# First batch of a fused attention and SwiGLU kernel: other PSUM banks for the turned rows and the late o, gates begun inside the fourth row's turn, late statistics moved to just behind the gates

## The chip, the cores and the metric

The kernel runs on one core of one Trainium2 chip. The metric is the device time of one execution in microseconds. The kernel before took 319.64 us in the median of three runs (319.98, 319.64 and 319.4). TensorE is called PE, VectorE DVE, ScalarE ACT, GpSimd POOL and SyncE SP.

## What is computed

Eight batches of eight heads, 576 positions, head size 64, go through a linear attention (no softmax): k and v of a head are multiplied to a 64x64 matrix, q is multiplied with it, each head's row is scaled to unit root mean square and by a gain. The heads are put side by side (512 columns), scaled again by row, and go through a gated layer with 1536 hidden columns.

```python
def _attn_ref(q, k, v, g_norm):
    kv = np.einsum('bhsd,bhse->bhde', k, v)
    out = np.einsum('bhsd,bhde->bhse', q, kv)
    rms = np.sqrt(np.mean(out * out, axis=-1, keepdims=True) + 1e-06)
    return (out / rms * g_norm).astype(np.float32)

def _moe_ref(x, w_gate, w_val, w_out, rms_g):
    rms = np.sqrt(np.mean(x * x, axis=-1, keepdims=True) + 1e-06)
    xn = x / rms * rms_g
    g = xn @ w_gate
    silu = g * (1.0 / (1.0 + np.exp(-g)))
    val = xn @ w_val
    return (silu * val @ w_out).astype(np.float32)
```

## The kernel before

All matrix work is in bf16 with sums in fp32. A batch has 512 main positions, in four chunks of 128 (a chunk is called c), and 64 positions that remain; the remainders of all eight batches make a ninth group. Heads are taken in pairs, so there are four pairs (called j) of 128 columns; `P0` is pairs 0 and 1, `P1` pairs 2 and 3.

The first batch (b = 0) is written out by hand, because everything waits for it. It is cut into an early half (chunks 0 and 1) and a late half (chunks 2 and 3), so that the gated layer can begin with 256 positions while attention goes on with the others. For each half the steps are these:

- q is turned by TensorE (`qT_quads`, `qT_halves`) and copied to `qTs` by ScalarE or VectorE (`qT_out`, L377);
- `oT_mm` (L472) multiplies it with the k-v matrix to the turned attention output; ScalarE squares that (`sqT_`, L483);
- `stat_pairs` (L497) sums the squares over each head with tiny matmuls (4 columns each), and a row of small VectorE steps (`lead_chain` for the early half, `chain`, L562 to L580, for the late half) makes the scale `al` of each row and head;
- `o_pairs` (L439) computes the attention output once more, not turned, and `xna_pairs` (L449, VectorE) scales it;
- `xT_mm` (L621) turns the scaled rows with TensorE's transpose, `xT_out` (L631 on ScalarE, L633 on VectorE) copies them with a gain to `x`. `rows(j, ...)` does both for pair j of the early half.

The gated layer takes `x` in four steps s, one for each pair: a gate is four matmuls that add up in one bank. `gates(0, range(3), 0, 256)` (L775 on) runs the first three gates side by side, all three with step 0, then with step 1, and so on, in two banks of the pool `mm1` and one of `o2`; then ScalarE's silus. `gate_of` and `val_of` (matmuls at L750) do one gate or one value product; the value product's end is VectorE's `h = silu * value` (L770). The list `early` holds these for the first 256 positions: the three gates, values 0 to 2, gates 3 to 5, values 3 to 5, gates 6 to 8, values 6 to 8, and so on. `lead` emits them one by one and calls `behind(n)` after the n-th. The weights come in four blocks of three (`wg[0..3]`, `wv[0..3]`), loaded by the POOL queue in turn, gate and value.

Between these stand the late half's steps. Before the change, `val_of` called `behind_val(j)` between its matmuls and its product: behind value 0 the statistics and their chain, behind value 2 the late o and xna of `P0`. `behind(4)`, after gate 3, did the same for `P1`, and `behind(9)` turned the late rows.

PSUM has eight banks, split into three pools: `mm1` (3), `o2` (2) and `att` (3). A tile takes a bank that was released, in the order of the program, and its first writer waits for that bank's last reader. In the kernel before, row 0 and the late o of `P0` took the two `o2` banks, row 1 and row 3 shared one `att` bank, one after the other, and row 2 took `mm1`.

Every engine takes its own instructions in the order in which they are emitted. From the second batch on, a planner (`Placer`) puts attention's steps into the slots of the gated layer by costs; it and its costs are not touched.

Of the kernel before, what the change touches and what calls it, by code (L numbers as in the profile page):

```python
# [14 lines left out]
OP = mybir.AluOpType  # L15
# [72 lines left out]
def kernel(  # L88
# [12 lines left out]
    nc = tc.nc  # L101
# [31 lines left out]
    o2_p = pool("o2", 2, space=bass.MemoryType.PSUM)  # L133
# [19 lines left out]
    wg = [consts.tile([128, NS, w * 128], BF16, name=f"wg{n}") for n, w in enumerate(FB)]  # L153
    wv = [consts.tile([128, NS, w * 128], BF16, name=f"wv{n}") for n, w in enumerate(FB)]
# [108 lines left out]
    class Att:  # L263
# [58 lines left out]
        def kv_half(self, half):  # L322
            rows, cols = slice(half * D, (half + 1) * D), slice(half * D, (half + 1) * D)
            nc.vector.tensor_copy(out=self.kv[rows, :, half, :], in_=self.kv_ps[rows, :, cols])  # L324

        def qT_quads(self, part, halves, pools):
            tiles = [
                pool.tile([128, 2, MAIN // 2], BF16, name="o2" if pool is o2_p else "att") for pool in pools
            ]
            for c in range(NC):  # L330
                for h in range(H // 2):
                    for ps, hh in zip(tiles, halves):
                        rows, at = slice(hh * D, (hh + 1) * D), slice(h % 2 * D, (h % 2 + 1) * D)
                        nc.tensor.matmul(
                            ps[at, h // 2, c * D : (c + 1) * D],
                            lhsT=mains[0, 0][rows, part, h, c * D : (c + 1) * D], rhs=ident[rows, rows],
                            is_transpose=True, start=True, stop=True, skip_group_check=True,
                        )
            return tiles
# [398 lines left out]
    hs = {}  # L738

    def x_of(g, s, c0, c1):  # L740
        if g == B:
            return xr[:, s, c0:c1]
        cs = slice(c0 // 128, c1 // 128)
        return xs[g][:, s, cs, :] if g < 2 else xs[g][:, cs, s, :]

    def mm1(g, w, j, c0, c1, name="mm1"):
        ps = {"mm1": mm1_p, "o2": o2_p, "att": att_p}[name].tile([128, MAIN], FP32, name=name)
        n, jj = where[j]
        for s in range(NS):
            nc.tensor.matmul(  # L750
                ps[:, : c1 - c0], lhsT=w[n][:, s, jj * 128 : (jj + 1) * 128], rhs=x_of(g, s, c0, c1), start=s == 0, stop=s == NS - 1
            )
        return ps[:, : c1 - c0]

    sis = {}

    def silu_of(g, j, ps, c0, c1):
        sis[g, j] = silu_p.tile([128, MAIN], BF16, name="silu")
        nc.scalar.activation(out=sis[g, j][:, c0:c1], in_=ps, func=ACT.Silu)  # L759

    def gate_of(g, j, c0=0, c1=MAIN):
        silu_of(g, j, mm1(g, wg, j, c0, c1, "o2" if g == 0 and c0 == 0 and j == 5 else "mm1"), c0, c1)

    def val_of(g, j, c0=0, c1=MAIN):
        if (g, j) not in hs:
            hs[g, j] = h_p.tile([128, MAIN], BF16, name="h")
        v_ps = mm1(g, wv, j, c0, c1, {0: "o2", 2: "att", 3: "o2"}.get(j, "mm1") if g == 0 and c0 == 0 else "mm1")
        if g == 0 and c0 == 0:
            behind_val(j)
        nc.vector.tensor_tensor(out=hs[g, j][:, c0:c1], in0=sis[g, j][:, c0:c1], in1=v_ps, op=OP.mult)  # L770

    def slots_a(g, j, c0=0, c1=MAIN):
        return [Slot("gate", lambda: gate_of(g, j, c0, c1)), Slot("val", lambda: val_of(g, j, c0, c1))]

    def gates(g, js, c0, c1):  # L775
        of = [(mm1_p, "mm1"), (mm1_p, "mm1"), (o2_p, "o2")]
        ps = [pool_.tile([128, MAIN], FP32, name=name)[:, : c1 - c0] for _, (pool_, name) in zip(js, of)]
        for s in range(NS):
            for p, j in zip(ps, js):
                n, jj = where[j]  # L780
                nc.tensor.matmul(
                    p, lhsT=wg[n][:, s, jj * 128 : (jj + 1) * 128], rhs=x_of(g, s, c0, c1), start=s == 0, stop=s == NS - 1
                )
        for p, j in zip(ps, js):
            silu_of(g, j, p, c0, c1)
# [97 lines left out]
    V, G, A = nc.vector, nc.gpsimd, nc.scalar  # L883
    H0, H1 = (0, 4), (4, 8)
    P0, P1 = (0, 1), (2, 3)
# [36 lines left out]
    a = Att(0)  # L922
# [7 lines left out]
        a.kv_pairs_out(kva, i, j)  # L930
    idle_on(mains[0, 0][:D, 0, 0:2].rearrange("p h x -> p (h x)"), 1)
    qa, qb = a.qT_quads(0, (0, 1), (att_p, att_p))
    a.qT_out(qa, P0, 0, A)
    a.qT_out(qb, P1, 0, V)
    gT = o2_p.tile([128, NS + 1], FP32, name="o2")
    nc.tensor.matmul(gT, lhsT=grow, rhs=identf, is_transpose=True, start=True, stop=True, skip_group_check=True)
    kvc = a.kv_pairs((2,))
# [10 lines left out]
    for half in range(2):  # L948
        rows = slice(half * D, (half + 1) * D)
        V.tensor_tensor(out=sel[rows, 1, half : half + 1], in0=gcol[rows], in1=gcol[rows], op=OP.mult)  # L950
    V.tensor_scalar(
        out=gain, in0=gall[:, 0:NS], scalar1=gcol, scalar2=float(d_model) ** 0.5, op0=OP.mult, op1=OP.mult
# [12 lines left out]
            a.xna_pairs(o[:, :, 2 * i : 2 * i + 2], (j,), 0, 2)  # L965

    def rows(j, pool_, eng):
        a.xT_mm((j,), (0, 1), ps=xt[j] if j == 0 else a.xT_ps(1, (0, 1), pool_))
        a.xT_out(j, (0, 1), eng)

    xt = [a.xT_ps(1, (0, 1), o2_p)]
    lo = [a.oT_mm(P0, 2, 4, o2_p)]
    rows(0, None, A)
    rows(1, None, A)
    lo.append(a.oT_mm(P1, 2, 4))
    for ps, js in zip(lo, (P0, P1)):
        a.sqT_(ps, js, 2, 4)
    A.preload_act_table(ACT.Silu)
    rows(2, mm1_p, V)
    rows(3, None, V)  # L980

    for t in (0, 2, 1):
        load_cast(1, t, (0, H))
# [11 lines left out]

    half = MAIN // 2
    early = [Slot("half", lambda: gates(0, range(FB[0]), 0, half))]
    for n, w in enumerate(FB):
        js = range(FB0[n], FB0[n] + w)
        early += [slots_a(0, j, 0, half)[0] for j in js if n] + [slots_a(0, j, 0, half)[1] for j in js]  # L1000
    held = {}

    def late_rows(n):
        js = (P0, P1)[n]
        a.xna_pairs(a.o_pairs(js, 2, 4, att_p, "att"), js, 2, 4)

    def behind_val(j):
        if j == 0:
            a.st = None
            a.stat_pairs(P0, 2, 4, att_p, "att")  # L1010
            a.stat_pairs(P1, 2, 4, att_p, "att")
            for f in a.chain(2, NC):
                f()
        if j == 2:
            late_rows(0)

    def behind(n):
        if n == 4:
            late_rows(1)
        if n == 9:  # L1020
            for js in (P0, P1):
                a.xT_mm(js, (2, 3))
                for j in js:
                    a.xT_out(j, (2, 3), A)

    def lead(n0, n1):
        for n in range(n0, n1):
            if n == 12:
                gate = nc.sync.dma_start(out=gbc, in_=g_norm.partition_broadcast(128))
                tc.add_manual_dep(gate.ins, w_loads[-1][0].ins.name, SYNC, reason="the weights come first")  # L1030
            emit([early[n]])
            behind(n)
# [74 lines left out]
```

## Time and profile before

| | |
|---|---|
| median of the runs | 319.64 us (319.4 to 319.98) |
| the profiled execution's own time | 319.01 us |
| its span, from first to last instruction | 317.2 us |
| granted TensorE clock, mean | 1.000 |
| k of the first batch lands at | 7.93 us |
| first gate's matmul starts at | 16.83 us |
| PE is without a pause from | 25.52 us |

The profiled execution is one of many; durations are read from it. A timeline row gives start and length in microseconds, engine, line, operation, tiles written and read, their sizes, the count of instructions put together in the row, and in brackets the idle time of the engine before it with what ended it. Matmuls overlap in a pipeline: each takes a slot of its number of columns and ends some 0.16 us after that slot, so a row of two that shows 0.38 holds PE for 0.22.

### The profile page before, as it was taken

How to read it: one execution, taken by the hardware profiler on the slowest of the kernel's cores; microseconds unless marked ns; L12 is line 12 of the kernel's file. 1: busy time of each engine (PE TensorE's matmuls, PEld its weight loads, DVE VectorE, ACT ScalarE, POOL GpSimd, SP SyncE). 2: the span in 40 equal slices, each digit the busy share in tenths (PEclk: the TensorE clock that was granted, in tenths of full speed). 3: DMA queues.
4: the chain of work that ended last, by engine and by line, in shares of the span. 5: the costliest groups of instructions: out<-in, count | busy, mean ns of one | idle time of the engine just before them, and what ended most of it. 6: DMA issues, size and time to landing. Idle time of an engine off the chain costs nothing.

```text
span 317.2 us, 5713 instructions
## 1 busy us (share of the span) xinstructions
PE 308.0 (97%) x2205; PEld 156.1 (49%) x2226; DVE 168.0 (53%) x378; ACT 139.6 (44%) x264; POOL 87.1 (27%) x108
## 2 busy tenths in 40 slices
PE   7899999999999999999999999999999999999995
PEld 2578855544454445444544444444544444444443
DVE  4674546579759643854196618461769034103310
ACT  2365374596477324631483237322842233233321
POOL 8836430067018302820085008400510000000000
PEclk9999999999999999999999999999999999999999
DMA  8999999999853965595339855964001600040002
GB/s 195 197 203 199 196 238 198 190 217 143 194 177 58 190 156 159 107 192 133 123 98 147 158 147 131 161 139 131 2 0 25 192 1 2 21 106 5 2 33 99
DMA packets 78358, 40.18 MB, mean 127 GB/s; under 512 B 43000, under 2 KB 73852, under 8 KB 78332
## 3 DMA queue, kind: packets, MB, share of 16 engines
q0 software_dynamic: 32304, 14.75, 36.6%
q1 hardware_dynamic: 45328, 24.48, 30.9%
q10 hardware_dynamic: 700, 0.59, 0.6%
q8 instruction: 17, 0.28, 0.4%
q14 instruction: 9, 0.07, 0.1%
HBM read 37.78 MB, written 9.44 MB: 149 GB/s over the span
## 4 chain that ended last, share of the span: by engine, by line
PE 93%; DMA 2%; DVE 2%; issue 1%; ACT 1%; SPq 0%
PE mm L750 57%; PE o L788 27%; DMA stg<-in_k_dram 2%; PE mm L788 2%; PE att L294 2%; PE o L422 1%; PE att L422 1%; DVE h L770 0%; PE mm L312 0%; PE att L621 0%; ACT x L631 0%; PE mm L819 0%; PE o L819 0%; PE att L472 0%; PE o L750 0%
## 5 line engine op out<-in xcount | busy, mean ns | idle before, releaser
L770 DVE TENSOR_TENSOR h<-silu,mm 128x512 bf16<-128x512 bf16 (+1 forms) x117 | 74.3, 636 | 88.0 <-PE mm L750 79.1
L759 ACT ACTIVATE silu<-mm 128x512 bf16<-128x512 f32 (+1 forms) x118 | 65.7, 560 | 83.8 <-PE mm L750 73.4
L750 PE MATMUL mm<-x,wv 128*128 128x512 bf16 (+1 forms) x418 | 97.8, 358 | 0.2
L750 PE MATMUL mm<-x,wg 128*128 128x512 bf16 (+1 forms) x414 | 97.3, 358 | 0.2
L788 PE MATMUL o<-wo,h 128*128 128x512 bf16 x382 | 87.5, 379 | 1.1 <-issue 0.6
L750 PEld LDWEIGHTS <-wv 128*128 128x128 bf16 x480 | 46.4, 98 | 45.7 <-issue 0.5
L750 PEld LDWEIGHTS <-wg 128*128 128x128 bf16 x468 | 45.5, 98 | 46.2 <-issue 0.2
L514 POOL TENSOR_TENSOR sq<-sq,g 128x512 bf16<-128x512 bf16 x28 | 32.0, 1154 | 127.5 <-ACT sq L405 81.9
L788 PEld LDWEIGHTS <-h 128*128 128x128 bf16 x420 | 40.3, 98 | 47.0
L808 ACT COPY osb<-o 128x512 f32<-128x512 f32 x33 | 19.3, 587 | 69.1 <-PE o L788 66.2
L522 DVE TENSOR_REDUCE st<-sq 128x8 f32<-128x512 bf16 x56 | 35.9, 678 | 0.0
L324 DVE CAST kvs<-att 64x256 bf16<-64x256 f32 x14 | 5.9, 422 | 30.7 <-PE att L294 30.5
L591 DVE TENSOR_TENSOR xna<-outa,al 128x512 bf16<-128x512 bf16 x24 | 15.1, 682 | 0.0
L750 PE MATMUL mm<-xr,wv 128*128 128x512 bf16 x47 | 12.3, 379 | 0.1
L750 PE MATMUL mm<-xr,wg 128*128 128x512 bf16 x47 | 12.3, 379 | 0.1
L229 POOL CAST main_q<-stg 128x1024 bf16<-128x1024 f32 x10 | 10.2, 1068 | 0.0
L908 ACT ACTIVATE wv<-wv,gain 128x384 bf16<-128x384 bf16 x16 | 9.0, 607 | 0.4 <-PE mm L750 0.4
L200 POOL DMA_DIRECT2D vc<-in_v_dram x10 | 8.5, 859 | 2.1 <-PE att L359 1.1
L788 PE MATMUL mm<-wo,h 128*128 128x512 bf16 x23 | 7.4, 379 | 0.2 <-issue 0.2
L459 ACT ACTIVATE sq<-att 128x512 bf16<-128x512 f32 x12 | 7.6, 630 | 0.0
L459 ACT ACTIVATE sq<-o 128x512 bf16<-128x512 f32 x12 | 7.3, 610 | 0.0
L200 POOL DMA_DIRECT2D kc<-in_k_dram x7 | 6.5, 933 | 2.7 <-DMA kc<-in_k_dram 1.6
(150 smaller groups left out, 186.9 us busy)
## 6 DMA issues: line engine op xcount, KB each, us to landing
out_dram<-osb SPq DMA_DIRECT2D x27, 256.0 KB, 2.5
stg<-in_q_dram SPq DMA_DIRECT2D x6, 1024.0 KB, 7.5
vc<-in_v_dram POOLq DMA_DIRECT2D x7, 512.0 KB, 8.1
kc<-in_k_dram POOLq DMA_DIRECT2D x7, 512.0 KB, 6.2
out_dram<-osb SPq DMA_DIRECT2D x17, 128.0 KB, 2.4
wg<-in_moe_w_gate_dram POOLq DMA_DIRECT2D x4, 384.0 KB, 10.2
wv<-in_moe_w_val_dram POOLq DMA_DIRECT2D x4, 384.0 KB, 11.4
wo<-in_moe_w_out_dram POOLq DMA_DIRECT2D x4, 384.0 KB, 14.4
```

The lines of the kernel that those rows point to most:

```text
L200: return nc.gpsimd.dma_start(out=to[:, heads[0] : heads[1], : NC * D], in_=view)
L229: return copy(out=mains[b, t][:, cs[0] : cs[1], h0:h1, :], in_=staged[b, t].rearrange("p h (c d) -> p c h d", c=NC)[:, cs[0] : cs[1], h0:h ...
L459: nc.scalar.activation(out=self.sq[c][:, 0], in_=self.o_of(c), func=ACT.Square)
L514: eng.tensor_tensor(out=self.sq[c][:, 1], in0=self.sq[c][:, 0], in1=g2, op=OP.mult)
L522: nc.vector.reduce_sum(out=self.part(self.st[:, which], c), in_=of, axis=AX.X)
L591: return eng.tensor_tensor(out=self.part(self.xna, c), in0=of, in1=self.part(self.al, c).to_broadcast([128, 2, H // 2, D]), op=OP.mult,)
L750: nc.tensor.matmul(ps[:, : c1 - c0], lhsT=w[n][:, s, jj * 128 : (jj + 1) * 128], rhs=x_of(g, s, c0, c1), start=s == 0, stop=s == NS - 1)
L759: nc.scalar.activation(out=sis[g, j][:, c0:c1], in_=ps, func=ACT.Silu)
L770: nc.vector.tensor_tensor(out=hs[g, j][:, c0:c1], in0=sis[g, j][:, c0:c1], in1=v_ps, op=OP.mult)
L788: nc.tensor.matmul(ps, lhsT=hs[g, j][:, t * 128 : (t + 1) * 128], rhs=wo[j // OB][:, j % OB, :], start=j == 0, stop=j == NF - 1)
L808: (eng.copy if eng is nc.scalar else eng.tensor_copy)(out=o, in_=ps)
L908: A.mul(out=w[:, s], in_=w[:, s], mul=gain[:, s : s + 1])
```

## The change

Five things are changed, all in the first batch's early part:

- The two copies of the early q swap engines: the half for `P0` goes to VectorE, that for `P1` to ScalarE.
- Rows 0 and 1 both take `o2` banks; the late o of `P0` takes an `att` bank in place of `o2`, and stands behind row 0.
- Row 3 is no longer turned ahead of the gates but inside `gates`, after the three matmuls of step 0.
- The statistics of the late half and their chain stand right behind the gates, ahead of value 0's matmuls. The late o and xna of `P0` stand behind value 2's matmuls as before, but value 2's product on VectorE is held back (`held`) until xna of `P1` has been emitted.
- Gate 7 of the early half takes an `o2` bank (gate 5 already did).

```diff
     def gate_of(g, j, c0=0, c1=MAIN):
-        silu_of(g, j, mm1(g, wg, j, c0, c1, "o2" if g == 0 and c0 == 0 and j == 5 else "mm1"), c0, c1)
+        silu_of(g, j, mm1(g, wg, j, c0, c1, "o2" if g == 0 and c0 == 0 and j in (5, 7) else "mm1"), c0, c1)
 
     def val_of(g, j, c0=0, c1=MAIN):
...
-        v_ps = mm1(g, wv, j, c0, c1, {0: "o2", 2: "att", 3: "o2"}.get(j, "mm1") if g == 0 and c0 == 0 else "mm1")
-        if g == 0 and c0 == 0:
-            behind_val(j)
-        nc.vector.tensor_tensor(out=hs[g, j][:, c0:c1], in0=sis[g, j][:, c0:c1], in1=v_ps, op=OP.mult)
+        leads = g == 0 and c0 == 0
+        v_ps = mm1(g, wv, j, c0, c1, {0: "o2", 2: "att", 3: "o2"}.get(j, "mm1") if leads else "mm1")
+
+        def product():
+            nc.vector.tensor_tensor(out=hs[g, j][:, c0:c1], in0=sis[g, j][:, c0:c1], in1=v_ps, op=OP.mult)
+
+        if leads and j == 2:
+            held["product"] = product
+        else:
+            product()
...
         for s in range(NS):
+            if s == 1:
+                rows(3, None, V)
             for p, j in zip(ps, js):
...
-    a.qT_out(qa, P0, 0, A)
-    a.qT_out(qb, P1, 0, V)
+    a.qT_out(qa, P0, 0, V)
+    a.qT_out(qb, P1, 0, A)
...
     def rows(j, pool_, eng):
-        a.xT_mm((j,), (0, 1), ps=xt[j] if j == 0 else a.xT_ps(1, (0, 1), pool_))
+        a.xT_mm((j,), (0, 1), ps=a.xT_ps(1, (0, 1), pool_))
         a.xT_out(j, (0, 1), eng)
 
-    xt = [a.xT_ps(1, (0, 1), o2_p)]
-    lo = [a.oT_mm(P0, 2, 4, o2_p)]
-    rows(0, None, A)
-    rows(1, None, A)
+    rows(0, o2_p, A)
+    lo = [a.oT_mm(P0, 2, 4)]
+    rows(1, o2_p, A)
     lo.append(a.oT_mm(P1, 2, 4))
...
     rows(2, mm1_p, V)
-    rows(3, None, V)
...
-    def behind_val(j):
-        if j == 0:
+    def behind(n):
+        if n == 0:
             a.st = None
             a.stat_pairs(P0, 2, 4, att_p, "att")
             a.stat_pairs(P1, 2, 4, att_p, "att")
             for f in a.chain(2, NC):
                 f()
-        if j == 2:
+        if n == 3:
             late_rows(0)
-
-    def behind(n):
         if n == 4:
             late_rows(1)
+            held.pop("product")()
```

## The prediction, made before the changed kernel ran

> **What bounds the kernel now.** I read the page first, then the busy time by stretches of the span, then the chain of waits from 14 to 40 us, then the timeline of the four engines over the same stretch, and last the landings of the loads. The page says TensorE:
>
> ```profile
> span 317.2 us, 5713 instructions
> ...
> PE 308.0 (97%) x2205; PEld 156.1 (49%) x2226; DVE 168.0 (53%) x378; ACT 139.6 (44%) x264; POOL 87.1 (27%) x108
> ...
> PE 93%; DMA 2%; DVE 2%; issue 1%; ACT 1%; SPq 0%
> ```
>
> The share is an average. The next two rows are of the busy time by stretches (first the stretch and its length, then PE, PEld, DVE, ACT, POOL busy with counts, then the granted clock, the DMA share, GB/s):
>
> ```profile
> 14.40:25.52 11.12, 9.72 (x101) 7.82 (x99) 7.71 (x27) 8.26 (x20) 5.75 (x10) 1.00 1.31 203
> 25.52:39.20 13.68, 13.68 (x130) 12.09 (x132) 6.69 (x16) 5.87 (x16) 7.23 (x11) 1.00 1.45 197
> ```
>
> From 25.52 us on PE is full. Ahead of that, where the change works, it idles 11.12 - 9.72 = 1.40 us, and every microsecond taken out there moves the rest of the kernel forward, unless a load is late. The chain names who ends those waits (start, length, engine, tile, line):
>
> ```profile
> 16.72 0.27 PE att L621 x2
> ...
> 18.30 0.44 PE o L750 x4
> 18.74 0.19 PE att L497 x8
> ...
> 18.96 0.18 DVE u L562
> ...
> 21.42 0.42 DVE h L770
> ...
> 21.89 0.60 PE o L750 x4
> ...
> 23.61 1.08 DVE h L770 x3
> ...
> 25.52 13.70 PE mm L750 x124
> ```
>
> Read it so: the fourth row (L621) comes late, the gates follow it, then the first value product (L750, 0.44), then the statistics (L497), which start a run of twelve small VectorE steps; only behind them stands the first h (21.42), whose bank the fourth value product (21.89) wants. Later VectorE, then ScalarE, hold PE until 25.52.
>
> **The change part by part.** All times below are of the profiled execution. Lags come from the rows: about 0.03 from PE's end to ScalarE or VectorE, 0.05 back; a 256-column matmul takes 0.44/4 = 0.11, so a group of four 0.44 and twelve gates 1.31; a 128-column one half.
>
> *The swapped q copies.*
>
> ```profile
> 10.87 0.59 ACT L377 COPY qTs<-att 128x512 bf16<-128x512 bf16 x1 [3.11 <-PE att L334]
> 10.90 0.42 DVE L377 COPY qTs<-att 128x512 bf16<-128x512 bf16 x1 [0.42 <-PE att L334]
> 11.51 0.38 PE L472 MATMUL o<-qTs,kvs 128*128 128x256 bf16 x2
> 11.94 0.27 PE L472 MATMUL o<-qTs,kvs 128*128 128x256 bf16 x1
> ```
>
> ScalarE ends at 11.46 and PE starts the first o 0.05 later. With VectorE on that half the copy ends at 11.32 and PE starts at 11.37: 0.14 gained. The bounds are 0 (PE is held by the products ahead) and 0.17 (the two durations' difference); I take 0.14, because 11.46 + 0.05 is just when PE starts. The other half now ends at 11.49, still ahead of its reader at 11.94 - 0.14. Statistics, scale and xna of the first half follow in a chain without slack, so I move all of them by 0.14.
>
> *Rows and gates.*
>
> ```profile
> 15.03 1.42 DVE L449 TENSOR_TENSOR xna<-att,al 128x256 bf16<-128x256 f32 x4
> 15.51 0.28 PE L621 MATMUL o<-ident,xna 128*128 128x128 bf16 x2
> 15.83 0.47 ACT L631 ACTIVATE x<-o,gain 128x256 bf16<-128x256 bf16 x1 [0.23 <-PE o L621]
> 16.20 0.47 ACT L631 ACTIVATE x<-att,gain 128x256 bf16<-128x256 bf16 x1
> 16.49 0.35 DVE L633 TENSOR_SCALAR x<-mm,gain 128x256 bf16<-128x256 bf16 x1
> 16.56 0.60 ACT L483 ACTIVATE sqT<-o 128x512 bf16<-128x512 f32 x1
> 16.83 0.38 PE L781 MATMUL mm<-x,wg 128*128 128x256 bf16 x2
> 17.04 0.61 ACT L483 ACTIVATE sqT<-att 128x512 bf16<-128x512 f32 x1
> 17.66 1.28 ACT L978 ACT_TABLE_LOAD   x1
> ```
>
> Before, row 3 took the bank of row 1 and so waited for ScalarE's second x (16.20 + 0.47 = 16.67; PE at 16.72), and all gates stood behind it. After, rows 0 and 1 have the two o2 banks, row 3 one that only needs its own data, and the first gate of each of the three banks asks for x of row 0 alone. Worked forward: xna ends at 15.31, 15.64, 15.98, 16.31 (15.03 - 0.14, 0.33 apart, 0.42 long); row 0 on PE 15.37 to 15.65; ScalarE's x0 15.69 to 16.16, x1 0.37 behind it, to 16.53; gates of step 0 from 16.20, three of them; row 3 16.53 to 16.81; step 1 at 16.64 (x1 is there), step 2 at 16.97 (x2, 16.35 + 0.35), step 3 at 17.30 (x3, 16.84 + 0.35 = 17.19). The last gate is issued by 17.62. So the gates begin 16.83 - 16.20 = 0.63 earlier, of which 0.14 is the copy, and give 0.11 back for row 3's two transposes. The weight changes around these have no row; bounds are 0 and two loads, 0.2, and I take 0, since PEld overlaps PE throughout.
>
> *Statistics ahead of the first value product.* They need both late squares: ScalarE's order stays x0, x1, square, square, so the second ends at 16.42 + 0.48 + 0.61 = 17.51, in time for 17.62. Statistics then end at 17.62 + 0.16 (a matmul's tail) + 0.19 = 17.97 and VectorE starts at 18.00 in place of 18.96: 0.96 = 0.14 + 0.38 + 0.44 for the value product taken out of the way. The table load moves with the squares to 17.52, the first silu to 18.80; the first h comes later than that and hides it.
>
> *The late half on VectorE.*
>
> ```profile
> 22.09 0.68 DVE L449 TENSOR_TENSOR xna<-att,al 128x512 bf16<-128x512 f32 x1
> 23.20 0.39 PE L621 MATMUL att<-ident,xna 128*128 128x128 bf16 x4
> 23.62 1.57 ACT L631 ACTIVATE x<-att,gain 128x256 bf16<-128x256 bf16 x4 [1.63 <-PE att L621]
> 23.98 2.13 PE L750 MATMUL mm<-x,wg 128*128 128x256 bf16 x16
> 25.06 1.47 ACT L759 ACTIVATE silu<-mm 128x256 bf16<-128x256 f32 x4
> ```
>
> The small steps take 21.42 - 18.96 = 2.46, so h 0 is 20.46 to 20.87, and value 3 could start at 20.92. PE by itself gets there at 17.62 + 0.19 + six groups of 0.44 + two late o of 0.22 = 20.89. Then h 1, xna of the first pair 21.13 to 21.81, and now at once xna of the second, 0.60 behind: 22.41, because h 2 stands behind it. PE's late turns at 22.26 and 22.48 wait for neither; before, the second waited. Held back, h 2 starts at 22.33 and h 3, 4, 5 follow 0.33 apart, the last until 23.73. The next gates that take their banks come at 23.8 and 24.2, so some 0.4 of cover is left; without it PE would wait for that rest. Gate 7 in an o2 bank waits for a silu in place of h 4. ScalarE takes the late x from 22.26 + 0.39 + 0.03 = 22.68; its silus start 1.44 behind, the third of them (0.36 apart, 0.38 long) ends at 24.12 + 0.72 + 0.38 = 25.22, and the second gate of the second half, which takes its bank, starts at 25.27. Before, that gate stood eight matmuls into the full stretch, at 25.52 + 0.88 = 26.40: 1.13 gained.
>
> *The loads.* No DMA is added, removed or moved on any queue, so landings stay put while PE comes nearer. Issue times and delays, of wg 1 to 3, of wv 1 alone, and of the last values' piece for batch 2:
>
> ```profile
> L248 POOL DMA_DIRECT2D wg<-in_moe_w_gate_dram x3: 760/780/797, 10.1 to 13.0; - x3
> ...
> DMA to landing us min/median/max: 9.1/11.4/13.8
> ```
>
> ```profile
> L249 POOL DMA_DIRECT2D wv<-in_moe_w_val_dram x1: 770/770/770, 10.8 to 10.8; - x1
> ...
> DMA to landing us min/median/max: 10.1/10.1/10.1
> ```
>
> ```profile
> L196 POOL DMA_DIRECT2D vc<-in_v_dram x1: 692/692/692, 42.5 to 42.5; - x1
> ...
> DMA to landing us min/median/max: 15.6/15.6/15.6
> ```
>
> ```profile
> 11.51 0.78 POOL L248 DMA_DIRECT2D wg<-in_moe_w_gate_dram  x1
> 59.17 0.82 PE L294 MATMUL att<-vc,kc 128*64 128x64 bf16 x40
> ```
>
> wg 1 lands at 19.2, wanted after the change at 17.62 + 0.19 + 1.32 + 0.22 = 19.35. wv 1 lands at 20.9: value 3 at 20.95, a gain of 0.94 there. wg 2 lands at 11.51 + 11.4 = 22.9, so gate 6 starts at 22.95 and not 22.70: 23.98 - 22.95 = 1.03. The values' piece lands at 58.1 and is wanted eight matmuls into the row at 59.17, 0.15 later: no gain past 59.32 - 58.15 = 1.17 survives this place.
>
> **Sum.** By the weights' gate 1.03, by ScalarE's silus 1.13; I take the middle, 1.07 (to 0.01, by hand). The profiled execution took 319.01 us, span 317.2 and 1.81 around it; it becomes 317.94. The runs' median is 319.64, 0.63 over it, so the same step gives 319.64 - 1.07 = **318.6 us**.
>
> **The rivals.**
> *Loads clip the gain.* The early start is real, but wg 2 or the values' piece lands some 0.3 to 0.7 later against PE than in this one execution, and PE waits. For it: the room left is 0.15, 0 and 0, where 0.7 to 1.1 was before, and the DMA share is above 1 in both stretches. Against: the landings follow each other on a full queue, and nothing of this change touches it. Gain 0.4 to 0.8, 319.0, about half of it within 0.2%.
> *The gates do not begin early.* ScalarE's x0, or PE's order, holds step 0 until row 3 is turned, and the swap is covered. Then only the statistics' place is left, 0.44: 319.2. For it: PE takes its queue in order, so any late x between the steps stops all. Against: the x times above, each 0.03 or more ahead of use.
> *Slower, by the clock.* The denser mix of transposes, tiny statistics and half-filled steps from 14 to 25 us lets the granted clock fall there. Price: the stretch's 9.72 us of PE at clock c costs 9.72/c - 9.72; the gain is eaten at 0.90, and below 0.85 (1.72) the kernel is slower than can be told from no change; at 0.75 it is 3.24 - 1.07 slower, 321.8. Against: the clock is 1.00 in the same stretch, which already has these transposes and more idle time.
> The Trainium skill, "TensorE: Matmul & The Clock Gate", Part 4, says that transposes do not count as PE work for the clock gate as matmuls do, which is this rival's rule; this trace shows 1.00 with them, so it does not bear it out.
>
> **How the numbers follow.** Forecast 0.66, loads 0.18, no early gates 0.08, clock 0.08. What a measurement of this kernel can tell from no change is 0.2%, 0.64 us. Faster is the forecast and half of the loads' case, 0.75; within is the other half and the third, 0.17; slower 0.08. The range starts from the gains 1.17 and 0.4 (318.5 and 319.2) and adds the spread of the runs' median, about 0.3 either way (319.4 to 319.98), with 0.2 more below for the lags: 318.0 to 319.5.
>
> **What would show it.** In the changed profile: PE's first o near 11.37; the first gates at 16.2 with row 3's turn inside them; VectorE's u at 18.0; value 3 at 20.95; gate 6 at 22.95, its wait ended by a DMA or not at all; no wait for VectorE ahead of the second late turn; PE full from about 25.3, and the second batch's values product near 58.1 without a wait. A u later than 18.5, a wait of PE on h 4 or 5, a wait on a load over 0.3 us, or a clock under 1.00 would make the prediction wrong.

## The result, and the profile after

The changed kernel took 317.78 us in the median of seven runs (317.57 to 318.6), the kernel before 319.34 us in the median of seven beside them (318.76 to 319.98). The ratio is 0.9957 with an interval of [0.9943, 0.9972]: 1.56 us or 0.49% less, more than the 0.2% that can be told from no change. The profiled execution took 317.84 us, 1.17 less than the 319.01 of the one before. The forecast was 318.6, and the time lies below its range.

The page of the kernel after, its span, its busy times and its chain's shares by engine:

```profile
span 316.1 us, 5734 instructions
...
PE 309.8 (98%) x2226; PEld 156.0 (49%) x2226; DVE 167.8 (53%) x378; ACT 139.5 (44%) x264; POOL 87.1 (28%) x108
...
PE 92%; DMA 5%; POOL 1%; issue 0%; DVE 0%; ACT 0%; POOLq 0%
```

The span is 1.1 shorter, and VectorE and ScalarE have left the chain that this page counts. The stretch ahead of the full one, by busy time (columns as before):

```profile
14.40:25.52 11.12, 10.31 (x107) 8.68 (x108) 7.54 (x28) 8.56 (x21) 5.57 (x9) 1.00 1.31 203
```

PE idles 11.12 - 10.31 = 0.81 us there, where it idled 1.40, and that although 0.62 of the 0.81 (14.40 to 15.02) lies ahead of the first row. The chain of waits of the kernel after, from 14 to 40 us, shows who ends the rest:

```profile
10.16 10.84 DMA wv<-in_moe_w_val_dram
...
21.04 0.61 PE o L750 x4
...
22.98 0.61 PE mm L750 x4
```

The chain goes back from the fourth value product (21.04) to a load, wv 1, issued at 10.16, landed at 21.00. Ahead of that load the chain names nothing in this execution. Its timeline, by row (start, length, engine, line, tiles, sizes, count, idle time before with what ended it):

```profile
15.02 0.28 PE L621 MATMUL o<-ident,xna 128*128 128x128 bf16 x2 [0.90 <-DVE xna L449]
15.86 0.38 PE L789 MATMUL mm<-x,wg 128*128 128x256 bf16 x2
16.19 0.27 PE L621 MATMUL att<-ident,xna 128*128 128x128 bf16 x2
17.66 0.17 DVE L562 TENSOR_SCALAR u<-att 128x16 f32<-128x16 f32 x1 [0.81 <-PE att L497]
21.04 0.61 PE L750 MATMUL o<-x,wv 128*128 128x256 bf16 x4 [0.19 <-DMA wv<-in_moe_w_val_dram]
22.36 0.61 PE L621 MATMUL att<-ident,xna 128*128 128x128 bf16 x8
22.79 1.57 ACT L631 ACTIVATE x<-att,gain 128x256 bf16<-128x256 bf16 x4 [1.51 <-PE att L621]
22.98 0.61 PE L750 MATMUL mm<-x,wg 128*128 128x256 bf16 x4
25.23 0.60 PE L750 MATMUL mm<-x,wg 128*128 128x256 bf16 x4
```

The gates begin at 15.86 with row 3's turn (16.19) inside them; the statistics reach VectorE at 17.66; the eight late turns (22.36) go through without a wait; ScalarE's late x start at 22.79 and the second gate of the second half at 25.23. One thing grew: PE idles 0.90 us ahead of row 0, where it idled 0.54 ahead of the late o before.

Another execution of the same kernel, taken with e18_after, had v's last load later (11.67 in place of 11.18). The chain of waits of e18_after:

```profile
15.50 0.28 PE o L621 x2
...
20.76 0.92 PE o L750 x8
...
23.02 0.44 PE mm L750 x4
...
23.89 14.19 PE mm L750 x128
```

Here no load stands in the chain: from row 0 at 15.50 on it names PE alone. But a pause of PE shorter than 0.16 us lies under the modelled end of the matmul before it, and neither the busy time nor the chain shows it. The starts in the timeline of e18_after do:

```profile
22.81 1.57 ACT L631 ACTIVATE x<-att,gain 128x256 bf16<-128x256 bf16 x4 [1.19 <-PE att L621]
23.73 1.04 PE L750 MATMUL mm<-x,wg 128*128 128x256 bf16 x8
24.25 0.40 ACT L759 ACTIVATE silu<-mm 128x256 bf16<-128x256 f32 x1
24.71 0.60 PE L750 MATMUL mm<-x,wv 128*128 128x256 bf16 x4
24.78 0.69 ACT L759 ACTIVATE silu<-mm 128x256 bf16<-128x256 f32 x2
25.25 0.60 PE L750 MATMUL mm<-x,wg 128*128 128x256 bf16 x4
```

Eight matmuls from 23.73 hold PE until 24.60, and the next starts at 24.71, 0.06 behind the first silu (24.25 + 0.40); four from 24.71 hold it until 25.15, and the second gate of the second half starts at 25.25, 0.05 behind the third silu (24.78 to 25.20). So ScalarE ends the last two waits, 0.11 and 0.10. In the nine profiled executions of the changed kernel and its versions below that keep gate 7's bank and had no fall of the clock, this gate starts 2.43 to 2.45 behind ScalarE's first late x, whatever the head and the loads did. The changed kernel thus reaches its late turns by PE's own work when its head is late (22.39) and behind wv 1 when its head is early (22.36), ScalarE's silus set the start of the gate behind them, and both executions have the same span of 316.1 us.

### The profile page after: what moved, and what is told of

Same layout as the page of the kernel before. It is cut to its first block, busy times and chain, and to the rows that moved or that the text cites. A ratio compares the mean times of both kernels' runs of the same rounds, so it can differ in the third digit from the quotient of the medians.

```text
span 316.1 us, 5734 instructions
## 1 busy us (share of the span) xinstructions
PE 309.8 (98%) x2226; PEld 156.0 (49%) x2226; DVE 167.8 (53%) x378; ACT 139.5 (44%) x264; POOL 87.1 (28%) x108
## 4 chain that ended last, share of the span: by engine, by line
PE 92%; DMA 5%; POOL 1%; issue 0%; DVE 0%; ACT 0%; POOLq 0%
PE mm L750 58%; PE o L796 27%; DMA wv<-in_moe_w_val_dram 3%; DMA vc<-in_v_dram 2%; PE mm L796 2%; PE att L294 2%; PE o L422 1%; PE att L422 1%; PE att L621 0%; PE mm L827 0%; PE o L827 0%; PE o L750 0%; PE att L397 0%; PE att L472 0%; POOL remv L895 0%
## 5 line engine op out<-in xcount | busy, mean ns | idle before, releaser
L796 PE MATMUL o<-wo,h 128*128 128x512 bf16 x396 | 89.9, 379 | 0.0
```

Of the source, the lines that this page charges most:

```text
L796: nc.tensor.matmul(ps, lhsT=hs[g, j][:, t * 128 : (t + 1) * 128], rhs=wo[j // OB][:, j % OB, :], start=j == 0, stop=j == NF - 1)
```

## The experiments

In some runs the mean granted clock reads 0.995 or less. Two of them were profiled, and in both the clock had fallen for one or two stretches of 3.41 us in the first 20 us (a fall, below). These runs are counted apart in this table, since they are mostly 1 to 4 us longer. Each block of rows shares its runs of the kernel before.

| kernel | all runs, median us | clock 0.997 or more: median us | runs under 0.997 |
|---|---|---|---|
| before (beside e1 to e4) | 318.98 | 318.98 | 0 of 35 |
| e1_after | 318.60 | 317.75 | 6 of 12 |
| e2_swap | 318.96 | 318.94 | 1 of 11 |
| e3_stats | 318.32 | 318.31 | 2 of 11 |
| e4_rows | 318.36 | 318.33 | 1 of 12 |
| before (beside e5 to e8) | 319.06 | 319.06 | 0 of 34 |
| e5_spin | 318.07 | 317.98 | 1 of 10 |
| e6_spin_late_w | 318.22 | 318.22 | 0 of 11 |
| e7_before_late_w | 319.13 | 319.13 | 0 of 11 |
| e8_spin_split | 317.98 | 317.98 | 0 of 12 |
| before (beside e9 to e12) | 319.06 | 318.90 | 8 of 35 |
| e9_after | 318.32 | 318.04 | 4 of 12 |
| e10_spin_no_swap | 317.87 | 317.87 | 0 of 12 |
| e11_spin_no_hold | 318.01 | 317.96 | 1 of 12 |
| e12_spin_no_gate7 | 318.17 | 318.17 | 0 of 12 |
| before (beside e13 to e15) | 318.85 | 318.85 | 1 of 29 |
| e13_spin_before | 318.91 | 318.91 | 0 of 11 |
| e14_spin_rows | 318.57 | 318.57 | 0 of 11 |
| e15_spin_stats | 318.44 | 318.44 | 0 of 12 |
| before (beside e16 to e18) | 318.88 | 318.86 | 2 of 26 |
| e16_late_o_first | 318.31 | 318.07 | 4 of 12 |
| e17_filler_one | 317.98 | 317.98 | 0 of 8 |
| e18_after | 317.88 | 317.87 | 3 of 12 |

### The change whole, and its parts

e1_after is the changed kernel once more, beside three kernels with one part of the change each.

> The whole change again, beside the kernel before on the same chip. Theory (the terms are right, the miss came from carrying one execution's distance to a median of other runs): 1.07 us less than the kernel before, between 0.9 and 1.25, and the profiled execution shows the fourth value product waiting for the weights of block 1. Rival (the gain is larger than the summed terms, because the kernel before is also held by something that the profiled execution did not show): 1.35 us or more less.

Without falls it is 318.98 - 317.75 = 1.23 us less than the kernel before; with them the ratio is 0.999 [0.9973, 1.0007]. The six runs with a fall have a median of 319.49, 1.74 more than the other six. Its profile caught one (mean clock 0.995; two stretches by busy time, then PE's timeline):

```profile
11.92:15.33 3.41, 2.29 (x37) 1.58 (x35) 2.20 (x11) 1.87 (x6) 2.93 (x5) 1.00 1.31 203
15.33:18.74 3.41, 3.36 (x20) 2.60 (x21) 1.68 (x5) 2.88 (x6) 1.16 (x2) 0.50 1.32 204
```

```profile
15.38 0.39 PE L621 MATMUL o<-ident,xna 128*128 128x128 bf16 x2 [0.89 <-DVE xna L449]
16.84 0.63 PE L789 MATMUL mm<-x,wg 128*128 128x256 bf16 x2
```

The granted clock is 0.50 for 3.41 us from 15.33, and two gates' matmuls take 0.63 where they took 0.38. It begins where the idle piece ahead of row 0 ends, behind a stretch in which PE worked 2.29 of 3.41 us.

e2_swap has the swapped copies alone, in the kernel before.

```diff
-    a.qT_out(qa, P0, 0, A)
-    a.qT_out(qb, P1, 0, V)
+    a.qT_out(qa, P0, 0, V)
+    a.qT_out(qb, P1, 0, A)
```

> The kernel before with only the two q copies swapped between ScalarE and VectorE. Theory: 0.14 us less (the copy ends 0.14 earlier and everything behind it follows), bounds 0 and 0.17. Rival (part of the larger gain comes from here): 0.3 us or more less.

Its ratio is 1.0002 [0.9991, 1.0012]: no change, but 0.14 us would lie inside that interval too, so the timeline has to decide. That of e2_swap:

```profile
11.03 0.38 PE L472 MATMUL o<-qTs,kvs 128*128 128x256 bf16 x2
11.45 0.38 PE L312 MATMUL mm<-vc,main_k 128*128 128x128 bf16 x4
13.24 0.26 DVE L540 RECIPROCAL r<-mm 128x16 f32<-128x16 f32 x1 [0.58 <-PE mm L497]
```

and of the kernel before:

```profile
11.51 0.38 PE L472 MATMUL o<-qTs,kvs 128*128 128x256 bf16 x2
11.72 0.38 PE L312 MATMUL mm<-vc,main_k 128*128 128x128 bf16 x4
13.52 0.26 DVE L540 RECIPROCAL r<-mm 128x16 f32<-128x16 f32 x1 [0.49 <-PE mm L497]
```

Behind the first o PE multiplies the last heads' k and v (L312). That load landed at 11.41 in e2_swap and at 11.68 in the kernel before, and both times L312 starts 0.04 later and the first statistics step (r) 1.79 to 1.80 behind L312. In e2_swap PE was done with the first o at 11.03 + 0.22 = 11.25 and waited 0.20 for the load. An earlier q copy moves only the o in front of that wait.

e3_stats has the late statistics behind the gates alone, e4_rows the banks and row 3 inside the gates alone.

> The kernel before with only the late statistics and their chain moved from behind the first value product's matmuls to behind the gates. Theory: the chain's first step on VectorE comes 0.44 us nearer to the gates, the fourth value product follows it, 0.44 us less in all. Rival: more than 0.6 us less, or nothing, if the wait at the fourth value product is taken by something else.

> The kernel before with only the other banks for the rows and the late o, and row 3 turned inside the gates. Theory: the wait of row 3 for the second x of ScalarE is gone, two transposes are inside the gates: 0.32 to 0.38 us less. Rival (no early start, because the late o now waits for the second copy of ScalarE and holds the rows): 0 to 0.1 us less.

Ratios 0.9985 [0.9974, 0.9995] and 0.9987 [0.9977, 0.9998]. From r to u, where the statistics reach VectorE, the profiled executions take 5.44 us before (13.52 to 18.96), 5.00 in e3_stats and 5.08 in e4_rows: 0.44 and 0.36 less, as forecast. The medians, 0.67 and 0.65 under the kernel before, looked too large for that; e13 to e15 return to them.

### Does a filled idle piece keep the clock up, and do the loads decide?

e5_spin puts three matmuls that compute nothing into PE's idle piece ahead of row 0.

```diff
     oy = a.o_pairs(P1, 0, 2, att_p, "att")
+    spin(mm1_p.tile([128, MAIN], FP32, name="mm1"), 3)
```

> The changed kernel with three more 512-column matmuls into a bank of their own, behind the first half's last o and ahead of row 0's turn, where PE idles 0.90 us. Theory (the falls of the granted clock come from that idle piece): the runs have no fall, mean granted clock 0.999 or more, about 1.2 us less than the kernel before (ratio 0.996). Rival (the falls come from the mix of small matmuls as a whole): in a third to a half of the runs the mean granted clock is still near 0.995 and these are some 1.7 us longer. Third: the added matmuls end after row 0 is ready and cost what they stick out, up to 0.3 us, with no fall.

One run of ten fell (0.989); the others lie 1.08 under the kernel before. The filler pushes nothing back: row 0 starts 2.00 behind the first statistics step r in its profile (13.80 to 15.80), as in the kernel after (13.02 to 15.02).

e6_spin_late_w and e7_before_late_w delay the weights in e5_spin and in the kernel before, e8_spin_split brings their first columns early.

```diff
-    w_loads = [load_w(n) for n in range(len(FB))]
+    w_loads = [load_w(0)]
+    load_cast(1, 2)
+    w_loads += [load_w(n) for n in range(1, len(FB))]
...
-        if t:
+        if t == 1:
             load_cast(1, t)
```

> The kernel of e5_spin with one 64 KB piece of v's load moved ahead of the weights of pieces 1 to 3 on POOL's queue, so that these land later. Theory (the weights' landings set the end of the changed kernel): value 3 and gate 6 start as much later as wv 1 and wg 2 land, about 0.3 to 0.6, and the time is 0.3 to 0.6 us over e5_spin. Rival (VectorE's and ScalarE's chain sets it): within 0.1 of e5_spin.

> The kernel before with the same piece of v's load moved ahead of the same weights. Theory (in the kernel before the weights have 0.7 to 1.1 us of room): within 0.1 us of the kernel before, with no wait of PE on wv 1 or wg 2. Rival (the weights already decide there): 0.3 to 0.6 us slower.

> The kernel of e5_spin with the first 128 columns of wg 1, wv 1 and wg 2 loaded by transfers of their own ahead of the rest. Theory (these landings are the last thing that holds PE): value 3 starts when PE itself gets there, 0.1 to 0.2 earlier, and the time is 0.1 to 0.3 us under e5_spin. Rival (VectorE's held product or ScalarE's silus take their place): within 0.1. Against both: the extra transfers delay the later weights and the time is 0.1 to 0.4 over e5_spin.

Later weights cost the changed kernel 318.22 - 317.98 = 0.24, a little less than expected, and the kernel before 0.07. In the profiled execution of e7_before_late_w PE did wait for wv 1 and for wg 2, 0.2 us each, which had not been expected there; that cost the runs nothing that can be told. The chain of waits of e6_spin_late_w goes back to wg 2:

```profile
12.20 11.10 DMA wg<-in_moe_w_gate_dram
23.30 0.04 issue
23.34 0.61 PE mm L750 x4
```

Earlier weights bring nothing (317.98 both), as the rival had it: in the profiled executions of e5_spin and e8_spin_split no load ends a wait of PE behind row 0, and the two last pauses, 0.11 each, are those behind ScalarE's silus, as in e18_after. Where the weights are not delayed, a load ends a wait of some length only in executions whose head is early.

### The clock again, and the smaller parts

e9_after repeats the changed kernel on another chip; e10 to e12 take one part out of e5_spin each: the swap, the held product, gate 7's bank.

> The changed kernel once more, beside the kernel before on another occasion than e1_after. Theory (the idle piece ahead of row 0 lets the clock fall, whenever the clock's own period ends badly for it): two to six of some twelve runs at a mean granted clock of 0.995, these 1.5 to 1.9 us longer than the others; the others 1.1 to 1.3 less than the kernel before. Rival (the falls were those of one chip on one occasion): none, all runs between 317.5 and 318.1.

> The kernel of e5_spin with the two q copies on their old engines. Theory (PE's products behind the first o wait for v's last load, so an earlier q copy gains nothing): first late o 0.14 later, the rest the same, within 0.1 us of e5_spin, 0.9 to 1.1 less than the kernel before. Rival (the prediction's chain without slack): 0.14 slower than e5_spin.

> The kernel of e5_spin with the third value product issued by VectorE in its old place, between the two late xna. Theory (gate 6 waits for wg 2 and so has 0 to 0.3 of cover): the second late turn waits 0.3 on VectorE and the loss is 0 to 0.2 us. Rival (no cover): the second late turn and all behind it are 0.3 to 0.4 later, and so is the end.

> The kernel of e5_spin with gate 7 back in the bank that it had. Theory (its bank comes free with a held value product, some 0.3 late): gate 7 waits up to 0.3 on VectorE and the time is 0.1 to 0.3 us over e5_spin. Rival (ScalarE's silus hold the next gates for as long): within 0.1.

Four runs of e9_after fell, as expected, but here the kernel before fell too, in 8 of 35; and the runs without a fall gained 0.86, less than expected. e5_spin itself did not run on this chip: it lies 1.08 under its kernel before. The three versions here lie 1.03, 0.94 and 0.73 under theirs (318.90). So the swap is again worth nothing that can be told, the held product some 0.1 (in e11_spin_no_hold the second late turn waits 0.2 for VectorE, where 0.3 was expected), and gate 7's bank about 0.3 (318.17 - 317.87 = 0.30 beside e10_spin_no_swap); these are differences of medians, without intervals of their own. PE's timeline of e12_spin_no_gate7, where the first value product of that place starts at 25.12,

```profile
22.84 2.44 PE L750 MATMUL mm<-x,wg 128*128 128x256 bf16 x16
25.12 0.60 PE L750 MATMUL mm<-x,wv 128*128 128x256 bf16 x4
```

and of e10_spin_no_swap, where it starts at 24.64:

```profile
22.88 0.61 PE L750 MATMUL mm<-x,wg 128*128 128x256 bf16 x4
23.33 0.60 PE L750 MATMUL o<-x,wg 128*128 128x256 bf16 x4
23.77 1.04 PE L750 MATMUL mm<-x,wg 128*128 128x256 bf16 x8
24.64 0.60 PE L750 MATMUL mm<-x,wv 128*128 128x256 bf16 x4
```

### The two parts without falls between them

> The kernel before with the three matmuls of e5_spin in the same place. Theory (they only fill an idle piece of PE): the median within 0.2 us of the kernel before, no run under a mean granted clock of 0.997 where the kernel before beside it has some. Rival (they push row 0 back, as their end lies 0.1 to 0.3 past its data): 0.1 to 0.3 slower.

> The kernel of e4_rows (other banks, row 3 inside the gates) with the three matmuls of e5_spin. Theory (the prediction's terms): 0.3 to 0.4 us less than the kernel of e13_spin_before. Rival (the single part brings what the medians of e4_rows showed): 0.6 to 0.7 less.

> The kernel of e3_stats (late statistics ahead of the first value product) with the three matmuls of e5_spin. Theory (the prediction's terms): 0.4 to 0.5 us less than the kernel of e13_spin_before. Rival (the single part brings what the medians of e3_stats showed): 0.6 to 0.7 less, and with e14_spin_rows 1.2 to 1.4 together.

The filler itself does nothing to the kernel before: 318.91 against 318.85, ratio 1.0001 [0.9992, 1.001]. Against e13_spin_before the rows bring 0.34 and the statistics 0.47; the intervals of these kernels against the kernel before are some 0.3 and 0.45 us either way. Those are the prediction's terms (0.38 and 0.44), and the 0.65 and 0.67 of the earlier medians did not come again; why those were larger stays open.

### Who makes the falls?

> The changed kernel with the late o of the first two pairs ahead of row 0 again, as in the kernel before, in its new bank; nothing is added. Theory (the change makes PE's idle piece longer by putting this o behind row 0, and a fall follows a period of 3.41 us with too little PE work): the idle piece splits, the emptiest 3.41 us of PE ahead of 16 us have 2.5 us of work in place of 2.24, and of some twelve runs none or one falls under a mean granted clock of 0.997; row 0 and all behind it start no later; 0.9 to 1.2 us less than the kernel before. Rival (row 0 waits for the o): 0.1 to 0.2 longer than the runs of e18_after without a fall. Rival (the place of the o has nothing to do with falls): as many falls as in e18_after.

```diff
-    rows(0, o2_p, A)
     lo = [a.oT_mm(P0, 2, 4)]
+    rows(0, o2_p, A)
```

> The changed kernel with one matmul of 512 columns in the place of e5_spin's three. Theory (a threshold in PE's work in a period): the emptiest 3.41 us have about 2.5 us of work, and the falls are as rare as in e16_late_o_first. Rival (only a filled idle piece helps): a third of the runs fall, as in e18_after.

> The changed kernel, beside e16_late_o_first and e17_filler_one on the same chip. Theory: a quarter to a half of the runs at a mean granted clock of 0.995 or less, these 1.5 to 2 us longer; the others 0.9 to 1.2 less than the kernel before. Rival (the falls belong to single chips): none.

e16_late_o_first went the rival's way. Its timeline:

```profile
14.12 1.05 ACT L377 COPY qTs<-att 128x512 bf16<-128x512 bf16 x2
15.22 0.38 PE L472 MATMUL att<-qTs,kvs 128*128 128x256 bf16 x2 [1.04 <-ACT qTs L377]
15.44 0.39 PE L621 MATMUL o<-ident,xna 128*128 128x128 bf16 x4
```

The o starts 0.05 behind the second of ScalarE's two copies (14.12 + 1.05 = 15.17), though its own q is the first: in its new place it waits for the `att` bank that the second copy reads. So the idle piece becomes 1.04, row 0 starts 2.36 behind r (13.08) in place of 2.00, the time without falls is 0.20 over e18_after, and four of twelve runs fall. With its banks the change was right to put row 0 first. The emptiest 3.41 us of PE in the stretch ahead of the gates (from 10.5 us on), by busy time, in e16_late_o_first, in the kernel after, in e17_filler_one and in the kernel before:

```profile
11.80:15.21 3.41, 2.15 (x36) 1.64 (x36) 2.30 (x11) 2.08 (x6) 2.60 (x4) 1.00 1.32 203
```

```profile
11.60:15.01 3.41, 2.24 (x37) 1.58 (x35) 2.24 (x11) 2.00 (x6) 2.77 (x5) 1.00 1.30 200
```

```profile
11.55:14.96 3.41, 2.46 (x38) 1.66 (x38) 2.38 (x11) 2.06 (x6) 2.41 (x4) 1.00 1.31 197
```

```profile
13.35:16.76 3.41, 2.56 (x38) 1.64 (x38) 2.71 (x10) 2.11 (x6) 2.05 (x3) 1.00 1.32 203
```

These figures are each of one execution. The runs with a fall, whatever its place, are 4 of 12 at 2.15, 13 of 43 at 2.24 (the seven runs of the result had none), 0 of 8 at 2.46 and 11 of 159 at 2.56. The parts do not fit as well: e4_rows, at 2.24 too, fell in 1 of 12, and e2_swap, e3_stats and e7_before_late_w, at 2.55 to 2.56, in 3 of 33. The clearest comparison is the filler: the changed kernel and its versions with one or three matmuls of it fell in 2 of 77 runs, the changed kernel without it in 13 of 43.

## Why the prediction was wrong, step by step

*The gain was read about right, in part by luck.* The sum was 1.07. Without falls the changed kernel lies 1.23, 0.86 and 0.99 under the kernel before in the three repeats, 1.03 in the mean, and the profiled execution that the sum was made against became 317.84, where 317.94 was worked out. The sum took the middle of two waits that stand one behind the other (gate 6 by the weights 1.03, the second gate of the second half by ScalarE's silus 1.13; their middle is 1.08). The later one decides: that gate, at 26.40 before and forecast at 25.27, came at 25.23, 1.17 earlier, and at 25.25 in e18_after. That it came so near is luck: the late turns were 0.10 to 0.13 later than forecast (22.36 and 22.39 for 22.26), and the silus stood 0.26 apart where 0.36 was taken.

*The step that failed is the last of the sum:* "The runs' median is 319.64, 0.63 over it, so the same step gives 319.64 - 1.07 = 318.6". The median of the kernel before is 318.85 to 319.06 in five other sets of 26 to 35 runs, and 319.34 in the result's seven, of which the first three were the shown ones. So the profiled 319.01 was the typical execution, and the three runs stood high. Taken from 319.01 the sum gives 317.94, 0.16 over the measured 317.78. The spread of 0.3 added below the range was too small for this 0.63. Why the three runs stood high is open: neither their profiles nor their clocks are on record, so a late head or a fall of the clock may have made them (the kernel before with a fall took 319.41 to 322.61).

A late head need not carry over to the changed kernel. The step r starts at 13.02 in the profiled execution of the result and at 13.51 in that of e18_after, 0.49 later, and both spans are 316.1. In e13_spin_before, r is 0.37 later than in the kernel before (13.89) and the span 0.4 longer (317.6). But there are only a few such pairs, and the medians do not say how much of the runs' scatter the change takes up.

*The swapped q copies, 0.14:* wrong, nothing of it is seen (e2_swap, e10_spin_no_swap), the lower bound given, though for another reason: the chain behind the o was taken as one "without slack", and holds a wait for v's last load. The term is missing where it should be: in e18_after, whose head stands as in the kernel before (r at 13.51 and 13.52), the gates begin at 16.35 and u comes at 18.15, both 0.15 later than forecast.

*Rows and gates, 0.38 beyond the swap:* 0.36 from r to u, 0.34 in time. *Statistics, 0.44:* 0.44 and 0.47. Both together shorten r to u from 5.44 to 17.66 - 13.02 = 4.64, by 0.80 where 0.82 was forecast. That u came at 17.66 and not at 18.00 in the execution of the result is its early head.

*The late half:* the second late turn waits no more, as forecast; holding the product is worth some 0.1. Gate 7's bank, priced only as part of the chain to 25.27, is worth about 0.3.

*The loads:* value 3 was forecast at 20.95 and came at 21.04 behind wv 1, gate 6 at 22.95 and came at 22.98 behind wg 2. PE stood 0.34 ahead of value 3 (20.26 + 0.44 = 20.70 to 21.04), a little over the 0.3 that the prediction had named as a sign of being wrong; the 0.19 of the row leaves out the modelled end. As a rival, that the loads clip the gain, they cost 0.24 only where e6_spin_late_w delayed them. The values' piece of batch 2 clipped nothing.

*Slower, by the clock:* given 0.08, it came in 13 of 43 runs, and in none of those that gave the result. Its price was right: the stretch from 14.40 to 25.50 shows a clock of 0.85 in e1_after, for which the prediction's formula gives 1.72, and 1.74 was measured. Its place was wrong, as far as the runs show: a filler in the emptier piece of PE ahead of row 0 took nearly all falls away, though the dense mix from 14 to 25 us behind it stayed. Which part of the change makes the falls is not shown: e4_rows has the same idle piece and fell in 1 of 12, and e16_late_o_first did not make the piece shorter. The Trainium skill, "TensorE: Matmul & The Clock Gate", Part 1, describes a free-running window of 3413 ns and a clock of either half or full rate, and these runs agree: 3.41 us, 0.50 and 1.00. Its rule there, under "HAM oscillation", to leave no idle gap of PE over some 3.4 us, is not enough here: the longest idle piece in the period ahead of the fall is 0.89 us.

## What to carry to other kernels

Before a distance between one profiled execution and a short median is carried into a forecast, run the kernel before more often and ask which of the two is typical: three runs stood 0.6 to 0.8 over the usual median here. A distance that a late transfer makes may not carry over either, where the change moves the end to something else. Pauses of PE shorter than a matmul's modelled end are read from the starts, not from the busy time. A part that is hidden must be followed to the next thing that its consumer waits for; here the o came earlier and the next products' load did not. Where a change opens an idle piece of PE ahead of dense work, try to fill it (one or three idle matmuls): the changed kernel with such a filler, and without the swap, had no fall in twelve runs, where the changed kernel beside it had four. Its ratio to the kernel before, 0.9955 [0.9933, 0.9976], flatters it, since eight of those 35 runs had a fall; without them it is 318.90 - 317.87 = 1.03 us less.

## What had not been expected of the hardware

Both falls that were profiled came behind a period of 3.41 us in which PE had little work, without one long pause: 2.29 us of it in e1_after and 2.34 in e11_spin_no_hold (periods are counted from the first boundary in the clock record of each execution). But no threshold follows from that. In e3_stats a period with 2.34 was followed by no fall, and in e16_late_o_first not even one with less:

```profile
14.05:17.46 3.41, 2.25 (x25) 1.86 (x23) 2.37 (x7) 2.83 (x7) 1.62 (x3) 1.00 1.32 205
17.46:20.87 3.41, 3.41 (x42) 2.99 (x41) 2.42 (x13) 2.70 (x7) 0.84 (x2) 1.00 1.31 201
```

This measure counts the modelled end of each matmul as work. With 0.16 us taken off each, the periods ahead of the two falls are the emptiest in the first 24 us of all twenty profiled executions, about 1.4 and 1.55 us against 1.7 or more; that was worked out from the traces after the runs, rests on two falls, and no run tests it. The first boundary lies at another point of every execution (3.9 to 7.2 us), which would explain why the same kernel falls in some runs only; that is not shown. In e11_spin_no_hold the fall began in the head, ahead of the filler and of the rows, and lasted two periods (by busy time):

```profile
7.96:11.37 3.41, 2.34 (x49) 1.54 (x48) 1.05 (x4) 0.40 (x1) 2.61 (x4) 1.00 1.43 187
11.37:14.78 3.41, 3.24 (x28) 2.48 (x28) 1.10 (x6) 1.55 (x4) 3.02 (x5) 0.50 1.30 199
14.79:18.20 3.41, 3.41 (x31) 2.22 (x29) 2.44 (x9) 1.29 (x3) 1.76 (x2) 0.50 1.33 207
```

Why it held for the second period, behind 3.24 us of work at half rate, is open, and so is why the kernel before fell in 8 of 35 runs on one chip and in 3 of 124 on the others.
